# A third buffer for turned d h rows, a blockwise last store, four buffers for gate rows of s, and the gate's slope arithmetic moved to VectorE, in a gated state-space and feed-forward kernel

## The chip, the cores and the metric

The kernel runs on one core of a Trainium2 chip. The metric is the time of one execution on the device, in microseconds (us). A program on one core has no second die to compare with, so a run counts as slow only when it is over 1.5% above the fastest of its kernel. Ratios and their intervals use the other runs, the fast ones; the medians and ranges quoted beside them count every run. All profiles are of fast runs. Executions scatter: the kernel before, run 59 times beside the first experiments, had a median of 732.47 us between 726.08 and 739.44. Differences of a few us are therefore read from many rounds, never from one run.

In the lines of the profile PE is TensorE (matmuls), DVE VectorE, ACT ScalarE, POOL GpSimd and SP SyncE, which here only issues transfers; PEld is TensorE's loading of weights, and a q behind a name is that engine's queue of instructions. The span is the time from the first to the last instruction, and the granted clock is the share of TensorE's full clock that it was given.

## The reference

The program computes a gated block and all its gradients, for 2048 rows of 512 columns in bf16:

```python
def _fwd_reference(...):
    x  = A_u
    xn = _layernorm(x, axis=-1)
    s  = _A_ref(xn, A_re, A_im, B_re, B_im, C_re, C_im, log_dt, Dskip)  # long convolution + xn * Dskip
    g  = _silu(_B_ref(xn, B_w1, B_w2))     # silu(xn @ w1) @ w2, hidden width 1792
    return x + s * g

def reference(..., grad_out):
    _out, _vjp = jax.vjp(_f, A_u, A_A_re, ..., B_w1, B_w2)
    return (_out, *_vjp(grad_out))         # output and 11 gradients
```

Three pieces of the backward pass matter here. The gradient through the gate needs, for each element of the feed-forward output o, silu(o) and its slope ("gate rows"). The gradient d W1 (512 x 1792) is the product of xn with d h, the gradient of the hidden rows. It comes last, after d W2 and the gradient of the state-space part.

## The kernel before

Four parts are touched or argued about. The helper `k.st` is `nc.gpsimd.dma_start`: a store issued by GpSimd. `k.evb` casts a PSUM tile to bf16, on ScalarE in the lines shown (source line L44).

The gate rows (eight passes, two rows of tiles each). ScalarE makes silu and a tanh; GpSimd turns them into the terms of the slope; VectorE multiplies:

```python
for c in range(last):
    ...
    S = gp.tile([P, 3, 2, P], BF16, name="S", tag="S", bufs=2)
    nc.sync.dma_start(S[:]..., k.Sd[0:3, :, 256 * c:256 * c + 256]...)            # L589
    ...
    nc.scalar.activation(out=g[:], in_=src, func=ACT.Silu)                       # L593
    nc.scalar.activation(out=o, in_=src, func=ACT.Tanh, scale=0.5)               # L594
    TT(out=k.ds[:, ts, :], in0=G, in1=g[:], op=ALU.mult)                         # L595
    nc.gpsimd.tensor_scalar(out=o, in0=o, scalar1=-0.5, scalar2=0.5, ...)        # L597
    nc.gpsimd.tensor_scalar(out=g[:], in0=g[:], scalar1=1.0, scalar2=-1.0, ...)  # L598
    TT(out=o, in0=o, in1=g[:], op=ALU.mult)                                      # L599
    nc.vector.tensor_single_scalar(out=o, in_=o, scalar=1.0, op=ALU.add)         # L600
    TT(out=o, in0=o, in1=G, op=ALU.mult)                                         # L601
    ...
    TT(out=o3, in0=o3, in1=S[:], op=ALU.mult)                                    # L603
```

d W1, in seven column groups. Each needs two loads that turn (transpose) d h rows on their way from the chip's main memory, HBM. `bufs` is the number of buffers that a tile rotates through, so a load waits until the oldest one is free:

```python
for f in range(k.FT // 2):                                   # seven column groups
    dh = fw.tile([P, k.T, 2, P], BF16, name="dh_tok", tag="dh_tok", bufs=2)
    for j in range(2):
        nc.sync.dma_start_transpose(dh[:, :, j, :], k.DHd[2 * f + j])   # L949, 512 KB each
    ob = fw.tile([P, k.DK, 256], BF16, name="o10", tag="o10", bufs=2)
    for dk in range(k.DK):                                   # four blocks of 128 rows
        ps = ...
        for t in range(k.T):
            nc.tensor.matmul(out=ps[:], lhsT=k.xn[...], rhs=dh[:, t]..., ...)   # L954
        k.evb(ob[:, dk], ps[:])
        yield
    k.st(o10[:, :, 256 * f:256 * f + 256], ob[:])            # L958
```

d W2 loads h (`h_in`, L916) and turns it on TensorE (L118); its matmuls are L936. The state-space part runs beside it and loads turned rows of its own, `YT` (L725), for the matmuls L736. All these loads are issued by SyncE, one queue. The order of the end of the program is:

```python
fw = pool("fw")
dw = chained([gen_dw2(k, fw), gen_dw1(k, fw)])
paced(ssm, dw, 0.35)                                          # state-space part beside d W2
...
interleave([gen_ln_bwd(k, pool("lw", side="right")), dw], [1, 1])   # layer norm beside d W1
```

## Time and profile before

| | before |
|---|---|
| time, median of the first 3 runs (range) | 731.04 us (729.82 to 732.09) |
| span of the profiled run, mean granted TensorE clock | 728.0 us, 0.928 |
| first matmul of d W1, its length to the last matmul | 657.4 us, 62.5 us |
| from the end of the last cast to the end | 7.7 us |

The page of the profile gives busy time for each engine and then the busy share in 40 equal slices (18.2 us each) in tenths. PEclk is the granted TensorE clock in tenths of full speed:

```profile
PE 597.1 (82%) x5460; PEld 430.5 (59%) x5500; DVE 553.3 (76%) x1070; ACT 496.5 (68%) x671; POOL 107.4 (15%) x180
...
PE   0667968869999975669898999978898989988685
...
PEclk9877989989999995779899999999999999999798
```

No engine is near 100%. The last three slices, d W1, have TensorE at 6, 8 and 5 tenths and no other matmuls than these, and the sixteenth to eighteenth, the gate rows, at 5, 6 and 6. The prediction shows the lines of these two stages and of the last microseconds.

### The profile page before, as it was taken

To read this page: it belongs to the slowest core of one execution; us is meant where nothing else is said; L and a number is where in the kernel's file an instruction comes from. 1 tells how busy PE (TensorE), PEld (TensorE's weight loads), DVE (VectorE), ACT (ScalarE), POOL (GpSimd) and SP (SyncE) were. 2 spreads that over 40 slices of the span, in tenths; PEclk is the share of its full clock that TensorE was granted. 3 is DMA by queue.
4 is the path that set the end of the run, shared out by engine and by line. 5 is a ranking of instruction groups with operands and counts; after the bars stand their busy time and mean duration, and the time that the engine had idled before them with its cause. 6 is when DMAs were issued, how large, how long until landed. Compare 5 with 4: busy or idle time off the path is not lost.

```text
span 728.0 us, 13934 instructions
## 1 busy us (share of the span) xinstructions
PE 597.1 (82%) x5460; PEld 430.5 (59%) x5500; DVE 553.3 (76%) x1070; ACT 496.5 (68%) x671; POOL 107.4 (15%) x180
## 2 busy tenths in 40 slices
PE   0667968869999975669898999978898989988685
PEld 0535646555675653455575676757577767647574
DVE  6969997959978849886896999756896948369700
ACT  6767858769889866958688787646747756455221
POOL 2172200000011026600000000000002020232110
PEclk9877989989999995779899999999999999999798
DMA  9877857769769986569988975589969995379891
GB/s 291 307 171 198 248 182 207 285 146 289 299 166 285 356 267 162 186 150 261 314 208 260 240 225 193 155 221 195 236 159 246 210 259 129 110 239 209 215 216 55
DMA packets 207042, 159.26 MB, mean 219 GB/s; under 512 B 129024, under 2 KB 185344, under 8 KB 203392
## 3 DMA queue, kind: packets, MB, share of 16 engines
q1 hardware_dynamic: 193856, 135.29, 70.6%
q0 software_dynamic: 6224, 18.10, 6.9%
q10 hardware_dynamic: 6896, 4.98, 2.2%
q8 instruction: 43, 0.70, 0.4%
q14 instruction: 23, 0.19, 0.1%
HBM read 65.14 MB, written 62.26 MB: 175 GB/s over the span
## 4 chain that ended last, share of the span: by engine, by line
issue 52%; POOL 4%; DMA 3%; DVE 2%; ACT 2%; PE 1%; POOLq 0%; ACTq 0%; SPq 0%; DVEq 0%
POOL out_dram L939 1%; DMA out_dram<-gout 1%; DMA Gr<-in_grad_out_dram 1%; POOL out_dram L816 1%; DMA out_dram<-o 1%; POOL out_dram L958 1%; POOL out_dram L631 1%; DMA dB<-dA 1%; POOL out_dram L996 1%; DMA Kd<-KE 1%; ACT YD L594 1%; DVE ds L595 1%; ACT g L593 1%; DVE sp_in L332 0%; ACT dA L44 0%
## 5 line engine op out<-in xcount | busy, mean ns | idle before, releaser
L44 ACT CAST dA<-ps_s 128x1024 bf16<-128x1024 f32 x96 | 94.5, 1036 | 18.3 <-PE ps_s L298 9.8
L893 PE MATMUL ps_da<-doT,W 128*128 128x256 bf16 x448 | 61.3, 282 | 5.0 <-ACT doT L44 2.9
L310 PE MATMUL ps_i<-I,sp_in 128*128 128x256 bf16 x384 | 53.9, 287 | 13.8 <-ACT dK L44 7.0
L541 PE MATMUL ps_h<-XT,W 128*128 128x256 bf16 x448 | 63.0, 292 | 1.3 <-ACT hT L44 0.6
L44 ACT CAST o<-ps_w 128x256 bf16<-128x256 f32 (+1 forms) x42 | 18.4, 441 | 66.1 <-PE ps_w L954 38.7
L746 DVE TENSOR_TENSOR Tp<-Vb,Eb 128x1344 bf16<-128x1344 bf16 x64 | 52.1, 853 | 14.4 <-ACT Vb L44 7.6
L954 PE MATMUL ps_w<-dh_tok,xn 128*128 128x256 bf16 x448 | 52.0, 280 | 10.5 <-DMA dh_tok<-DHd 10.5
L558 PE MATMUL ps_o<-W,aT 128*128 128x512 bf16 x209 | 54.4, 393 | 4.1 <-ACT aT L549 2.9
L44 ACT CAST dB<-ps_i 128x1024 bf16<-128x1024 f32 x48 | 47.2, 1025 | 13.2 <-PE ps_i L310 10.9
L954 PEld LDWEIGHTS <-xn 128*128 128x128 bf16 x448 | 44.9, 101 | 17.7 <-issue 11.3
L310 PEld LDWEIGHTS <-sp_in 128*128 128x128 bf16 x384 | 37.4, 102 | 29.1 <-DVE sp_in L333 13.7
L893 PEld LDWEIGHTS <-W 128*128 128x128 bf16 x448 | 44.6, 101 | 15.6 <-issue 6.2
L904 PE MATMUL ps_dx<-W,dhT 128*128 128x512 bf16 x224 | 53.7, 379 | 0.0
L541 PEld LDWEIGHTS <-W 128*128 128x128 bf16 x448 | 46.0, 105 | 12.8 <-issue 2.7
L895 DVE SCALAR_TENSOR_TENSOR dhT<-dhT,ps_da 128x512 bf16<-128x512 bf16 x56 | 37.5, 683 | 16.5 <-PE ps_da L893 16.3
L936 PE MATMUL ps_w<-YD,a_tok 128*128 128x512 bf16 x211 | 49.3, 379 | 0.9 <-issue 0.3
L44 ACT CAST Vb<-ps_v 128x672 bf16<-128x672 f32 x64 | 42.3, 726 | 7.7 <-PE ps_v L736 7.7
L286 PEld LDWEIGHTS <-TF 128*128 128x128 bf16 x384 | 27.3, 104 | 24.9 <-issue 13.9
L419 ACT ACTIVATE sn<-V 128x1024 bf16<-128x1024 int32 (+3 forms) x40 | 34.8, 888 | 8.2 <-DVE V L417 8.0
L298 PE MATMUL ps_s<-dB,F 128*128 128x512 bf16 x95 | 37.9, 405 | 2.6 <-DMA dB<-dA 1.8
L297 PE MATMUL ps_s<-dB,F 128*128 128x512 bf16 x87 | 35.0, 409 | 5.4 <-DMA dB<-dA 3.5
L447 PEld LDWEIGHTS <-YD 128*128 128x128 bf16 x512 | 24.3, 101 | 24.3 <-DVE YD L434 12.7
(220 smaller groups left out, 1368.7 us busy)
## 6 DMA issues: line engine op xcount, KB each, us to landing
Yd<-YD SPq DMA_DIRECT2D x8, 1024.0 KB, 5.1
sp_in<-Ud SPq DMA_DIRECT2D x8, 1024.0 KB, 6.8
h_in<-Hd SPq DMA_DIRECT2D x14, 512.0 KB, 4.3
Ed<-E SPq DMA_DIRECT2D x8, 672.0 KB, 5.2
Eb<-Ed SPq DMA_DIRECT2D x8, 672.0 KB, 5.3
Hd<-hT POOLq DMA_DIRECT2D x8, 512.0 KB, 6.4
Ud<-dA SPq DMA_DIRECT2D x4, 1024.0 KB, 9.3
KXd<-dA SPq DMA_DIRECT2D x4, 1024.0 KB, 6.2
```

Of the source, the lines that this page charges most:

```text
L44: return self.nc.scalar.copy(out=out, in_=in_)
L297: nc.tensor.matmul(out=ps[:, 4 * u:4 * u + 4], lhsT=F2[:, m0], rhs=B[:, 0, g0:g0 + 4, :], start=True, stop=False)
L298: nc.tensor.matmul(out=ps[:, 4 * u:4 * u + 4], lhsT=F2[:, m1], rhs=B[:, 1, g0:g0 + 4, :], start=False, stop=True)
L310: nc.tensor.matmul(out=ps[:, g], lhsT=Y[:, c, g0 + g, :], rhs=k.I2[:, c].rearrange("p c m -> p (c m)"), start=(c == 0), stop=(c == 1))
L541: nc.tensor.matmul(out=ps[:, j], lhsT=k.W1[:, dk, ft * P:ft * P + P], rhs=XTv[:, :, dk, :], start=(dk == 0), stop=(dk == DK - 1))
L558: nc.tensor.matmul(out=ps[:], lhsT=aT[:, ft, t * P:t * P + P], rhs=k.W2[:, ft, :], start=(ft == 0), stop=(ft == FT - 1))
L746: k.nc.vector.tensor_tensor(out=Tp[:, c, :, r ^ c].rearrange("p e (q w) a -> p q w e a", w=2), in0=Vb[:, :, c].rearrange("p q w (e a) -> p ...
L893: nc.tensor.matmul(out=ps[:, j], lhsT=k.W2[:, ft, dk * P:dk * P + P], rhs=dTv[:, :, dk, :], start=(dk == 0), stop=(dk == DK - 1))
L895: nc.vector.scalar_tensor_tensor(out=dh[:, i0:i0 + 2, :], in0=dh[:, i0:i0 + 2, :], scalar=1.0, in1=ps[:], op0=ALU.add, op1=ALU.mult)
L904: nc.tensor.matmul(out=ps[:], lhsT=dhs[ft // 8][:, ft % 8, t * P:t * P + P], rhs=k.W1[:, :, ft * P:ft * P + P], start=(ft == 0), stop=(ft ...
L936: nc.tensor.matmul(out=ps[:], lhsT=at[:, t, :], rhs=k.do[:, t, :], start=(t == 0), stop=(t == k.T - 1))
L954: nc.tensor.matmul(out=ps[:], lhsT=k.xn[:, t, dk * P:dk * P + P], rhs=dh[:, t].rearrange("p j n -> p (j n)"), start=(t == 0), stop=(t == k ...
```

## The change

Its intent, as the diff reads, is to take away four waits. VectorE and GpSimd stop handing the slope back and forth. SyncE's queue no longer stops behind a load of S that has no buffer. TensorE no longer waits for the third group of turned d h. And the program no longer ends behind a large last store. The whole diff:

```diff
-        S = gp.tile([P, 3, 2, P], BF16, name="S", tag="S", bufs=2)
+        S = gp.tile([P, 3, 2, P], BF16, name="S", tag="S", bufs=4)
...
-        nc.gpsimd.tensor_scalar(out=o, in0=o, scalar1=-0.5, scalar2=0.5, op0=ALU.mult, op1=ALU.add)
-        nc.gpsimd.tensor_scalar(out=g[:], in0=g[:], scalar1=1.0, scalar2=-1.0, op0=ALU.mult, op1=ALU.add)
+        nc.vector.tensor_scalar(out=o, in0=o, scalar1=-0.5, scalar2=0.5, op0=ALU.mult, op1=ALU.add)
+        nc.vector.tensor_scalar(out=g[:], in0=g[:], scalar1=1.0, scalar2=-1.0, op0=ALU.mult, op1=ALU.add)
...
-        dh = fw.tile([P, k.T, 2, P], BF16, name="dh_tok", tag="dh_tok", bufs=2)
+        dh = fw.tile([P, k.T, 2, P], BF16, name="dh_tok", tag="dh_tok", bufs=3)
...
             k.evb(ob[:, dk], ps[:])
+            if f == k.FT // 2 - 1:
+                nc.sync.dma_start(o10[:, dk, 256 * f:256 * f + 256], ob[:, dk])
             yield
-        k.st(o10[:, :, 256 * f:256 * f + 256], ob[:])
+        if f < k.FT // 2 - 1:
+            k.st(o10[:, :, 256 * f:256 * f + 256], ob[:])
```

## The prediction

> **What bounds the kernel now.** I began with the page. No engine is full: TensorE is busy 82% of a 728.0 us span, VectorE 76%, ScalarE 68%, GpSimd 15%. So the kernel is a sequence of stages with different limits, and I read the three stages that the diff touches in the views of waits, of time order and of single lines. Of its 40 slices (18.2 us each) those that matter are the sixteenth to eighteenth (273 to 328 us), where the granted TensorE clock falls to 0.5 to 0.7 because TensorE starves, and the last three.
>
> First the end. This is TensorE in order of time over the last 71 us, all of it d W1 (L954):
>
> ```profile
> 657.35 14.14 PE L954 MATMUL ps_w<-dh_tok,xn 128*128 128x256 bf16 x128
> 680.18 16.61 PE L954 MATMUL ps_w<-dh_tok,xn 128*128 128x256 bf16 x128 [8.69 <-DMA dh_tok<-DHd]
> 697.87 7.15 PE L954 MATMUL ps_w<-dh_tok,xn 128*128 128x256 bf16 x64 [1.08 <-DMA dh_tok<-DHd]
> 705.76 14.13 PE L954 MATMUL ps_w<-dh_tok,xn 128*128 128x256 bf16 x128 [0.74 <-DMA dh_tok<-DHd]
> ```
>
> One of the seven column groups is 64 matmuls, 7.07 us at full clock (14.14 / 2). The brackets are idle time and its releaser: 8.69 + 1.08 + 0.74 = 10.5 us lost to turned loads. The second row takes 16.61 us where 14.14 would do: after the long wait the clock is granted at 0.50 (680.0 to 683.5) and 0.86 (683.5 to 690.0) by the view of stretches, 2.5 us more. The loads sit on SyncE's queue:
>
> ```profile
> 664.53 5.19 SPq L949 DMA_TRANSPOSE dh_tok<-DHd  x1
> 669.82 0.53 SPq L974 DMA_DIRECT2D Gt<-in_grad_out_dram  x1
> 670.44 0.38 SPq L972 DMA_DIRECT2D pd_l<-Pd  x1
> 670.87 4.74 SPq L949 DMA_TRANSPOSE dh_tok<-DHd  x1
> ```
>
> Groups 0 and 1 were loaded long before (566 to 587 us). The third group's first load is issued at 664.5, just when group 0's matmuls end (657.35 + 7.07 = 664.4): it waits for one of two buffers. The second half leaves at 670.87 and lands at 680.2, 9.3 us later.
>
> Then the last microseconds, the drains and semaphores of the program's end:
>
> ```profile
> L1175 POOLq DRAIN  x3: 40/93/6652, 720.6 to 727.7; - x3
> L1175 SPq DRAIN  x3: 7/7/7, 723.6 to 727.5; - x3
> ```
>
> The last cast ends at 720.3; GpSimd issues the last store at 720.60; it lands 2.5 us later and SyncE, which waits for it, goes on at 723.6. But GpSimd's own drain, begun behind that store, lasts 6.65 us, to 727.3, and the end barrier follows. From the last cast to the end: 7.7 us, of which about 4 are the drain alone.
>
> Last the gate rows, 262 to 317 us, as groups of instructions and as waits:
>
> ```profile
> L599 DVE TENSOR_TENSOR YD<-YD,g 128x1024 bf16<-128x1024 bf16 x8 | 8.7, 1098 | 3.3 <-POOL g L598 2.4 <-POOL YD L597 0.9
> L597 POOL TENSOR_SCALAR YD<-YD 128x1024 bf16<-128x1024 bf16 x8 | 18.5, 2315 | 22.0 <-ACT YD L594 22.0
> L598 POOL TENSOR_SCALAR g<-g 128x1024 bf16<-128x1024 bf16 x8 | 9.8, 1229 | 9.0 <-DVE ds L595 9.0
> ```
> ```profile
> ACT g L593 <- DVE YD L599: 4.3, 1, 4.3
> ```
> ```profile
> 265.28 14.58 SPq L589 DMA_DIRECT2D S<-Sd  x3
> 279.95 5.09 SPq L288 DMA_TRANSPOSE dB<-dA  x2
> ```
>
> VectorE is busy 43.9 of the 47.4 us from 268.9 to 316.3, so it is the bound there, with its waits inside. L599's shortest run is 0.68 us, its mean 1.10. The third load of S cannot issue until 279.5, when the first L603 has freed one of its two buffers, and the turned loads of dA, whose first half ScalarE finished at 276.6, stand behind it.
>
> **What the skill says.** "SBUF — State Buffer", section "SBUF: two separate sides": GpSimd and VectorE share a port pair as an exclusive lock held for the whole instruction, taken from VectorE by ops in a two-port mode or with two SBUF inputs. The trace agrees: GpSimd's L597 lasts from 1.04 up to 9.58 us and VectorE's ops have a second length, 0.7 to 0.84 us longer. "VectorE: DVE Perf Modes", "The perf-mode tier table": a bf16 scalar op in SBUF runs at four elements a cycle, tensor by tensor at two. L600 (0.41 us) against L595 (0.68) of the same size agree. "DMA: Bandwidth & Descriptors", "SWDGE vs HWDGE vs iDMA": GpSimd's transfers have their descriptors built in software on GpSimd, SyncE's in hardware. The trace shows a 0.75 us issue for the L958 store on GpSimd and 0.3 to 0.5 us for plain SyncE copies; that this is what the long drain waits for is my inference. "TensorE: Matmul & The Clock Gate", "What's actually happening": an idle TensorE falls to half clock and needs about 3.4 us of work to be warm; the 0.50 above is that.
>
> **The change part by part.**
> *Slope arithmetic.* VectorE gains 16 ops like L600: 16 x 0.41 = 6.6 us. It loses the lock contention, mean minus undisturbed time times 8: L599 3.3, L595 1.7, L603 1.7, L601 1.0, L600 0.75, together 8.4 us; and the waits for GpSimd, 2.4 + 0.9 = 3.3. So 5.1 us less for VectorE in this stage.
> *Four buffers for S.* The queue is free at 276.6 instead of 279.9, and with the earlier release of g ScalarE's 4.3 us wait shrinks by perhaps 2; the last convolution's chain starts up to 4 us earlier. This overlaps with the 5.1: VectorE's total must be done before the next stage in any case. What passes on is the smaller of the two, with some idle time where VectorE now waits for ScalarE's activations. I count 4.5 for both. It moves everything after, since the backward convolution waits for L519 (4.0 us of "PE ps_s L286 <- DVE S_b L519") and no stage after works on anything ready earlier.
> *Third buffer of turned rows.* Group 2 is loaded before 657. TensorE runs groups 0 to 2 to 678.6 without a stop, at full clock. Group 3 takes the old places of group 2 in the queue (664.5, 670.9) and lands near 680.2: 1.6 us of waiting. Group 4 (queue places at 676.8 and 681, landing 686.7) is in time for 687.3. Groups 5 and 6 wait for buffers freed at 678.6 and 687.3 and need about 6 to 8 us of issue and 6.6 of landing: some 0.5 us each. The last matmul ends at 657.35 + 7 x 7.07 + 1.6 + 1.0 = 709.5 instead of 719.9: 10.4 us.
> *Price of it.* Two more turned loads go out near 585 to 604, where SyncE's queue is nearly always issuing (3 to 5 us for each or each pair) and the transfers' share is 1.14. TensorE there is busy 90% or more and has only one wait for a load (2.6 us, h_in at 590.8). The rows of Y for the next groups have 5 to 7 us in hand. I take 2 us as lost.
> *The end in blocks.* The seventh group's four blocks of 64 KB go out on SyncE, the first three during the matmuls. After the last cast: 0.2 to start, about 2.2 to land (the 128 KB stores of Pd need 1.7 at least), 0.8 of barrier: 3.2 instead of 7.7. GpSimd's last store is then group 5's, at about 703, and its drain is over by 710. 4.5 us.
>
> Sum: 4.5 + 10.4 - 2 + 4.5 = 17.4 us, from 731.0 to 713.6.
>
> **Rivals.**
> *The turned loads themselves become the bound.* Eight of them take 33.2 us from 676.8 to 710.0 on the queue, 8.3 us a pair, against 7.07 of matmuls. For it: the rate. Against: those pairs wait for buffers; the last three pairs take 5.0 to 6.8 us. If true, the last four groups run at 8.3: 4 x 1.2 = 5 us less gain, 718 to 719.
> *VectorE takes the place of GpSimd in the gate rows*, because the 16 ops come in between its products for the convolution. For it: 43.9 of 47.4 us. Against: it loses more contention than it gains work. Then this part gives 0, 718.
> *The early load collides* with the loads of Y and h, and TensorE stops 5 us instead of 2: 717. Against: at 604 to 640 the share is 0.34 to 0.54, so there is room if the order places it there.
> *The drain is fixed* and not tied to a store just issued: then it still begins earlier, after 703, so I give this little weight. If it waits for the last cast, the end gains 1 instead of 4.5.
> *Order.* The scheduler may order other work anew; that could be some us either way.
>
> **Range and chances.** The tail's two gains (14.9) are well founded and the limit of 2% is 716.4, so one failed part leaves it near the border. Predicted 714, range 707 to 722 in 8 of 10. Faster by over 2%: 0.70; within: 0.28; slower: 0.02.
>
> **What would show it.** Waits for dh_tok of 1 to 3 us instead of 10.5, a clock of 1.0 throughout the last 70 us, last matmul 10 us nearer to the first of d W1; 3 to 4 us between last cast and end, with SyncE's store as the last to land; no GpSimd arithmetic, L599 at 0.68 us, turned loads of dA right after the casts, d W1's first matmul about 2.5 us earlier (4.5 less 2). It is wrong if a wait for dh_tok above 5 us stays, if TensorE waits longer for loads between 580 and 610, or if d W1 starts no earlier than 657.

## The result, and the profile after

The changed kernel takes 712.42 us, median of 4 runs (711.24 to 713.23), against 731.27 us for the kernel before in the same rounds. The ratio is 0.9743, with a 95% interval of 0.972 to 0.9766. Ratios here are the mean time of one kernel's fast runs over that of the other's of the same rounds, so they are not quite the ratio of the medians quoted beside them. The gain is 0.0257 x 731.27 = 18.8 us; 17.4 was predicted. The profiled run's span is 711.3 us at a mean clock of 0.947.

The same three rows of the page, now of the kernel after (slices of 17.8 us):

```profile
PE 596.8 (84%) x5500; PEld 428.8 (60%) x5500; DVE 549.4 (77%) x1086; ACT 496.5 (70%) x671; POOL 79.0 (11%) x163
...
PE   0586978879999984769669899988899998999997
...
PEclk9879998999999996779999999999989999999999
```

The three last slices are now 9, 9, 7. TensorE's total work is about unchanged (597.1 and 596.8 us busy); the gain is idle time removed. GpSimd lost 107.4 - 79.0 = 28.4 us of work, which is the two lines of slope arithmetic of before (18.5 + 9.8).

TensorE in order of time in d W1, kernel after (start, length, line, tiles, count, and in brackets the idle time before and what ended it):

```profile
657.89 28.28 PE L954 MATMUL ps_w<-dh_tok,xn 128*128 128x256 bf16 x256
686.46 7.15 PE L954 MATMUL ps_w<-dh_tok,xn 128*128 128x256 bf16 x64 [0.29 <-DMA dh_tok<-DHd]
694.09 14.13 PE L954 MATMUL ps_w<-dh_tok,xn 128*128 128x256 bf16 x128 [0.48 <-ACT o L44]
```

Four groups (256 matmuls) run without a stop, where before two did. The waits for turned loads fell from 10.5 us to 0.3, and the clock between the first and the last matmul rose from 0.92 to 1.00. The stage takes 50.3 us instead of 62.5.

SyncE's queue, kernel after (start, length of the issue, line, tiles, count):

```profile
586.04 7.18 SPq L949 DMA_TRANSPOSE dh_tok<-DHd  x2
...
665.07 4.26 SPq L949 DMA_TRANSPOSE dh_tok<-DHd  x1
...
670.49 3.89 SPq L949 DMA_TRANSPOSE dh_tok<-DHd  x1
...
675.59 20.14 SPq L949 DMA_TRANSPOSE dh_tok<-DHd  x6
703.46 5.53 SPq L958 DMA_DIRECT2D out_dram<-o  x4
```

The pair at 586 is the third group, early. The pair at 665 and 670 has the queue places of before but now belongs to the fourth group, which TensorE wants only at 657.89 + 3 x 7.07 = 679.1. The last row is the end in blocks.

The drains at the end, kernel after (engine's sequencer, count, shortest/median/longest in ns, first and last start):

```profile
L1178 POOLq DRAIN  x3: 40/93/6573, 701.9 to 711.0; - x3
L1178 SPq DRAIN  x3: 7/7/7, 710.5 to 710.8; - x3
```

GpSimd's long drain is still 6.57 us, but it begins at 701.9 behind the sixth group's store and is over at 708.5, before the last cast ends (708.6). SyncE goes on at 710.5, when its last block has landed. From the last cast to the end it is 2.7 us instead of 7.7.

The gate rows, 262 to 312 us, as groups of VectorE's instructions, kernel after (line, form, count, busy us, mean ns, idle before):

```profile
L599 DVE TENSOR_TENSOR YD<-YD,g 128x1024 bf16<-128x1024 bf16 x8 | 5.5, 685 | 0.0
...
L597 DVE TENSOR_SCALAR YD<-YD 128x1024 bf16<-128x1024 bf16 x8 | 3.4, 421 | 2.2 <-ACT YD L594 2.2
...
L598 DVE TENSOR_SCALAR g<-g 128x1024 bf16<-128x1024 bf16 x8 | 3.3, 421 | 0.0
```

L599's mean fell from 1098 to 685 ns, the undisturbed length, and its waits for GpSimd are gone. The added ops cost 3.4 + 3.3 = 6.7 us; 6.6 was predicted. Two waits of the same stretch, and SyncE's queue there:

```profile
DVE ds L595 <- DMA Gr<-in_grad_out_dram: 5.2, 1, 5.2
...
ACT g L593 <- DVE YD L599: 4.0, 1, 4.0
```

```profile
267.06 10.51 SPq L589 DMA_DIRECT2D S<-Sd  x5
277.66 4.97 SPq L288 DMA_TRANSPOSE dB<-dA  x2
```

The turned loads of dA go out 2.3 us earlier than before (279.95). VectorE still waits before its first product, 5.2 us for the gradient's rows, where it waited 6.4 before, and ScalarE's wait of 4.3 us is still 4.0.

**A first reading, which fell.** These two profiles also seemed to say something else. In the time of the span, d W1's first matmul is at 657.4 before and 657.9 after. So the gate parts appeared to bring nothing: their lead was there at 305 us, where the last convolution of the forward pass ends, and was gone when d W1 began. I formed the theory that the lead is given back between 320 and 530 us, and that the tail alone brings the gain. The rival was the prediction's own account: the gate's gain arrives in the time, and the third buffer's price hides it at this one mark. The first four experiments were made to tell these apart.

### The profile page after: what moved, and what is told of

Read it like the earlier page. It is cut to its first block, busy times and chain, and to the rows that moved or that the text cites. A ratio compares the mean times of both kernels' runs of the same rounds, so it can differ in the third digit from the quotient of the medians.

```text
span 711.3 us, 13957 instructions
## 1 busy us (share of the span) xinstructions
PE 596.8 (84%) x5500; PEld 428.8 (60%) x5500; DVE 549.4 (77%) x1086; ACT 496.5 (70%) x671; POOL 79.0 (11%) x163
## 5 line engine op out<-in xcount | busy, mean ns | idle before, releaser
L310 PE MATMUL ps_i<-I,sp_in 128*128 128x256 bf16 x384 | 51.9, 279 | 12.2 <-DVE sp_in L333 6.2
L558 PE MATMUL ps_o<-W,aT 128*128 128x512 bf16 x224 | 57.2, 394 | 2.5 <-ACT aT L549 2.0
L904 PE MATMUL ps_dx<-W,dhT 128*128 128x512 bf16 x224 | 54.4, 385 | 0.3 <-DVE dhT L895 0.3
L936 PE MATMUL ps_w<-YD,a_tok 128*128 128x512 bf16 x224 | 51.8, 379 | 0.0
L954 PE MATMUL ps_w<-dh_tok,xn 128*128 128x256 bf16 x448 | 49.6, 273 | 0.8 <-ACT o L44 0.5
L297 PE MATMUL ps_s<-dB,F 128*128 128x512 bf16 x96 | 38.6, 409 | 8.7 <-ACT dA L44 4.2
L298 PE MATMUL ps_s<-dB,F 128*128 128x512 bf16 x96 | 37.7, 399 | 1.8 <-DMA dB<-dA 1.8
```

The costliest lines, as they stand in the source:

```text
L297: nc.tensor.matmul(out=ps[:, 4 * u:4 * u + 4], lhsT=F2[:, m0], rhs=B[:, 0, g0:g0 + 4, :], start=True, stop=False)
L298: nc.tensor.matmul(out=ps[:, 4 * u:4 * u + 4], lhsT=F2[:, m1], rhs=B[:, 1, g0:g0 + 4, :], start=False, stop=True)
L310: nc.tensor.matmul(out=ps[:, g], lhsT=Y[:, c, g0 + g, :], rhs=k.I2[:, c].rearrange("p c m -> p (c m)"), start=(c == 0), stop=(c == 1))
L558: nc.tensor.matmul(out=ps[:], lhsT=aT[:, ft, t * P:t * P + P], rhs=k.W2[:, ft, :], start=(ft == 0), stop=(ft == FT - 1))
L904: nc.tensor.matmul(out=ps[:], lhsT=dhs[ft // 8][:, ft % 8, t * P:t * P + P], rhs=k.W1[:, :, ft * P:ft * P + P], start=(ft == 0), stop=(ft ...
L936: nc.tensor.matmul(out=ps[:], lhsT=at[:, t, :], rhs=k.do[:, t, :], start=(t == 0), stop=(t == k.T - 1))
```

## The experiments

Three batches, each on one chip with the kernel before in the same rounds. The medians of before were 732.47 (59 runs), 731.44 (43 runs) and 731.92 us (35 runs). Gains in us are (1 - ratio) times that median. All results were correct. Of the experiments' runs 13 were slow and are left out of the ratios: one each of the gate parts alone, the end in blocks alone and the arithmetic alone, 4 of the 20 of the third buffer alone and 6 of the 20 of the whole last store from SyncE; so were 11 of the 137 of the kernel before. On one core this rule cuts the upper end of a plain scatter, and it cuts most where one run was unusually quick. With the means of all runs instead, the third buffer alone gains 6.7 us (7.6 by the ratio) and the whole store 4.1 (5.0); the others move by 0.9 us or less.

### Undo the gate parts

```diff
 (against the kernel after)
-        S = gp.tile(..., tag="S", bufs=4)
+        S = gp.tile(..., tag="S", bufs=2)
-        nc.vector.tensor_scalar(out=o, ...)
-        nc.vector.tensor_scalar(out=g[:], ...)
+        nc.gpsimd.tensor_scalar(out=o, ...)
+        nc.gpsimd.tensor_scalar(out=g[:], ...)
```

> The changed kernel with both gate parts undone (two buffers for S, slope arithmetic on GpSimd), third buffer of turned rows and the end in blocks kept. Theory T: in the changed kernel the second L519 comes 6.5 us earlier (306.96 instead of 313.42 us) but d W1 begins at 657.89 instead of 657.35, so the gate parts' lead is given back before 520 us and is worth nothing at the end. Then this kernel takes 712 to 714 us, as the changed one does, and its d W1 begins at 657 to 659. Rival C, the prediction's: the lead of some 4.5 us carries to the end and something else of the change costs as much between 460 and 657 us. Then this kernel takes 716 to 718 us.

Measured: 719.89 us (717.91 to 726.19, 6 runs), ratio 0.9837 (0.9784 to 0.989), a gain of 11.9 us where the full change has 18.8. The interval is wide, but the time is some 7 us above the kernel after. It is above both forecasts, and near what the third buffer and the end gain alone (7.6 + 4.5 = 12.1 us, below). The theory that the gate parts bring nothing does not fit.

### The gate parts alone

```diff
 (against the kernel before)
-        S = gp.tile(..., tag="S", bufs=2)
+        S = gp.tile(..., tag="S", bufs=4)
-        nc.gpsimd.tensor_scalar(...)      # both
+        nc.vector.tensor_scalar(...)      # both
```

> The kernel before with both gate parts (four buffers for S, slope arithmetic on VectorE) and nothing else. Theory T (lead given back): second L519 near 307 us, d W1 begins at 656 to 658, time 729.5 to 731.5 us, within 0.3% of before. Rival C (lead carried): d W1 begins near 652.5, time 726 to 727 us.

Measured: 726.99 us (22 runs), ratio 0.9933 (0.9909 to 0.9957), a gain of 4.9 us. This settles it: the interval excludes no gain. Its profile has the second half of the last convolution's output (L519; count, shortest/median/longest ns, first and last start) at 305.4 us:

```profile
L519 DVE TENSOR_TENSOR S_b<-ps_i,xd x8: 1217/1225/1232, 151.7 to 305.4; 128x1024 bf16<-128x1024 f32 x8
```

In the profile of before the same instruction starts at 313.4 us, and here d W1 does begin early, at 651.4 us.

### The third buffer alone

```diff
 (against the kernel before)
-        dh = fw.tile(..., tag="dh_tok", bufs=2)
+        dh = fw.tile(..., tag="dh_tok", bufs=3)
```

> The kernel before with the third buffer of turned rows alone. All engines but SyncE keep their order of instructions, so this is the part by itself. Expected by the prediction: waits for dh_tok 1 to 3 us instead of 10.5, last matmul 10 to 12 us earlier, less 0.8 us that the two earlier loads cost at 585 to 604 us; time 719 to 721 us. Rival, the turned loads become the bound at 8.3 us a pair: 724 to 726 us.

Measured: 726.76 us (20 runs), ratio 0.9896 (0.9868 to 0.9925), a gain of 7.6 us. TensorE in d W1, third buffer alone:

```profile
663.97 21.12 PE L954 MATMUL ps_w<-dh_tok,xn 128*128 128x256 bf16 x192
685.88 7.15 PE L954 MATMUL ps_w<-dh_tok,xn 128*128 128x256 bf16 x64 [0.79 <-DMA dh_tok<-DHd]
695.31 22.79 PE L954 MATMUL ps_w<-dh_tok,xn 128*128 128x256 bf16 x192 [2.29 <-ACT pd_l L988]
```

Three groups run through, then the fourth waits 0.8 us for its load. A wait of 2.3 us for ScalarE, which was at work for the layer norm, appears in place of later waits for loads. The stage is 54.1 us.

The time missed the forecast of 719 to 721 us. The rival that would give 724 to 726 is not what happened either, since TensorE's waits for turned loads fell to 0.8 us. What the forecast left out is this wait for ScalarE and the full price of the early loads, which it put at 0.8 us (see the last section of the experiments).

### The end in blocks alone

```diff
 (against the kernel before; as in the change)
+            if f == k.FT // 2 - 1:
+                nc.sync.dma_start(o10[:, dk, 256 * f:256 * f + 256], ob[:, dk])
...
+        if f < k.FT // 2 - 1:
+            k.st(o10[:, :, 256 * f:256 * f + 256], ob[:])
```

> The kernel before with the end stored in four blocks from SyncE and nothing else. If the 6.65 us drain of GpSimd behind its last store set the end: 5 us less, 725.5 to 726.5 us, 2.5 to 3 us from the last cast to the end of the span, and the long drain over before that. Rival, the landing of the store sets the end: 1 to 1.5 us less, 729.5 to 730 us.

Measured: 726.77 us (20 runs), ratio 0.9939 (0.9913 to 0.9965), a gain of 4.5 us. From the last cast to the end: 2.7 us, as in the full change.

The three parts alone add to 4.9 + 7.6 + 4.5 = 17.0 us (16.3 with the means of all runs), and together they give 18.8, with an interval of 17.1 to 20.5. They add, as far as this can be measured.

### Within the gate: the arithmetic alone

```diff
 (against the kernel before)
-        nc.gpsimd.tensor_scalar(...)      # both; S keeps 2 buffers
+        nc.vector.tensor_scalar(...)      # both
```

> The kernel before with the slope arithmetic on VectorE alone (S keeps two buffers). The two gate parts together gave a ratio of 0.9933 (4.9 us), and their profile began d W1 6 us earlier. If the lock with GpSimd is what cost the time: 3.5 to 5 us less, ratio 0.993 to 0.995, L599 at 0.68 us. Rival, the wait of SyncE's queue for S is what cost it: 0 to 1.5 us less.

Measured: 727.23 us (22 runs), ratio 0.9929 (0.9907 to 0.995), 5.2 us: all of what the two gate parts bring together.

The trace of the kernel before shows the lock at work. Two lines of it, of GpSimd and of VectorE:

```profile
275.21 1.47 POOL L597 TENSOR_SCALAR YD<-YD 128x1024 bf16<-128x1024 bf16 x1
275.70 1.52 DVE L599 TENSOR_TENSOR YD<-YD,g 128x1024 bf16<-128x1024 bf16 x1
```

Of the 40 VectorE instructions of L595, L599, L600, L601 and L603, 11 are longer than the shortest of their line, by 0.24 to 0.85 us, and each of the 11 began while a GpSimd instruction of 1.04 to 1.47 us was under way. Of the 29 that kept their shortest length, 23 began while neither L597 nor L598 ran. The other six began inside the one L597 that lasted 9.58 us, beside a row of VectorE instructions with hardly a gap: as this reads, there it was GpSimd that was held up.

This kernel does not separate the lock from the queue by time, since the turned loads of dA went out at 275.86 us instead of 279.95 here too. But TensorE waited for these loads only 1.4 us in the kernel before, and 3.6 us in this one.

### Within the gate: the four buffers alone

```diff
 (against the kernel before)
-        S = gp.tile(..., tag="S", bufs=2)
+        S = gp.tile(..., tag="S", bufs=4)
```

> The kernel before with four buffers for S alone (arithmetic stays on GpSimd). TensorE and GpSimd keep their order. If the lock with GpSimd cost the time: 0 to 1.5 us less, with the turned loads of dA issued at 276 to 277 instead of 279.95 us but VectorE as slow as before. Rival, the queue's wait cost it: 3.5 to 5 us less.

Measured: 729.08 us (22 runs), ratio 0.9979 (0.9953 to 1.0005), 1.5 us, not clear of zero. But the queue did not become free. SyncE's queue with four buffers for S alone:

```profile
265.18 14.70 SPq L589 DMA_DIRECT2D S<-Sd  x5
279.97 4.93 SPq L288 DMA_TRANSPOSE dB<-dA  x2
```

Four loads of S go out at once, but a fifth stands before the turned loads of dA. It leaves at 279.52 us, when the first L603 ends (279.5). So these loads are as late as in the kernel before, against the forecast. In the kernels with the moved arithmetic the first L603 ends earlier (at 275.4 us in the kernel with the arithmetic alone), and that is what lets them out. This experiment therefore shows that the buffers do little. It does not test what a freer queue alone would bring.

### The third group's early loads held back

GpSimd copies two columns of the tenth h load into the third buffer before its loads may write there, so these cannot go out before that load has landed. The values copied are overwritten by the loads, so the result stays correct.

```diff
 (against the kernel after)
         nc.sync.dma_start(h[:]..., k.Hd[ft])
+        if ft == 9:
+            k.flag = fw.tile([P, 2], BF16, name="flag", tag="flag", bufs=1)
+            nc.gpsimd.tensor_copy(out=k.flag[:], in_=h[:, 0, 0:2])
...
         dh = fw.tile(..., tag="dh_tok", bufs=3)
+        if f == 2:
+            nc.gpsimd.tensor_copy(out=dh[:, 0, 0, 0:2], in_=k.flag[:])
+            nc.gpsimd.tensor_copy(out=dh[:, 0, 1, 0:2], in_=k.flag[:])
```

> The changed kernel, but the third buffer's first two turned loads are held back until the tenth load of h has landed (a two-column copy on GpSimd stands before them), so that they go out after 604 us, when the rows of Y are all loaded, instead of at 586 to 593 us. If the early loads collide with those of Y and h, as the third buffer's traces hint (d W1 begins 6 us later in three of its profiles than in two without it, and 12.2 us of gain in the last stage became 7.6 in the time): 3 to 5 us less than the changed kernel of the same rounds. Rival, those late starts are scatter of single profiles and the price is 1 us or less: within 1 us of the changed kernel. In both cases no wait for dh_tok above 1 us.

Measured: 712.16 us (6 runs), ratio 0.9728 (0.9689 to 0.9767). The loads went out at 616.8 us instead of 583 to 593, and the stretch from d W2's first matmul to d W1's fell to 102.9 us. TensorE in d W1, loads held:

```profile
655.43 21.12 PE L960 MATMUL ps_w<-dh_tok,xn 128*128 128x256 bf16 x192
679.90 29.77 PE L960 MATMUL ps_w<-dh_tok,xn 128*128 128x256 bf16 x256 [3.35 <-DMA dh_tok<-DHd]
```

Starting earlier, TensorE outruns the fourth group's loads, which still wait for the first buffer, and stands 3.35 us. Neither theory expected this wait; both had said that none would be above 1 us. The price is gone and comes back as a wait, and the time moves by no more than the intervals allow for (712.16 against 713.11 us for the kernel after on the same chip).

### The kernel after again

```diff
 (no difference from the kernel after)
```

> The changed kernel once more, on the chip of these runs, since this batch's chip may scatter more than the first. All theories: 0.972 to 0.977 of before. Its profile is a second sample of where d W1 begins: with the price of some 4 to 5 us and the gate's gain of 5 us, 656 to 660 us; the sum of the parts measured alone (4.9 gate, 7.6 third buffer, 4.5 end) is 17 us, so a ratio near 0.976.

Measured: 713.11 us (6 runs), ratio 0.975 (0.9713 to 0.9788), 18.3 us: the result repeats on another chip. TensorE's waits between 560 and 658 us (total, times, longest) in this second profile of the kernel after:

```profile
PE ps_v L736 <- DMA YT<-Yd: 2.4, 2, 1.8
PE pt_t L118 <- DMA h_in<-Hd: 1.6, 1, 1.6
```

The first of them is not in the profile before. In the first profile of the kernel after it is not there either, and the wait for h_in is 1.8 us against 2.6 before. So a single profile does not show the price of the early loads reliably. All profiles together do (see the last section of the experiments).

### The last store whole, from SyncE

```diff
 (against the kernel before)
-        k.st(o10[:, :, 256 * f:256 * f + 256], ob[:])
+        (nc.sync.dma_start if f == k.FT // 2 - 1 else k.st)(o10[:, :, 256 * f:256 * f + 256], ob[:])
```

> The kernel before with the last store of d W1 whole (256 KB), only issued by SyncE instead of GpSimd. If the long GpSimd drain behind a last GpSimd store set the end: 7.7 us from last cast to end become 3 to 4 (issue 0.4 to 0.8, landing 2.5, barrier 0.8), 4 us less in the time. Rival, cutting the store into blocks is what gave the 5.0 us: here 0 to 1 us less.

Measured: 728.23 us (20 runs), ratio 0.9932 (0.9904 to 0.996), 5.0 us, or 4.1 with the means of all runs. From the last cast to the end 3.5 us.

### The last store in blocks, from GpSimd

```diff
 (against the kernel before)
+            if f == k.FT // 2 - 1:
+                k.st(o10[:, dk, 256 * f:256 * f + 256], ob[:, dk])
...
+        if f < k.FT // 2 - 1:
+            k.st(o10[:, :, 256 * f:256 * f + 256], ob[:])
```

> The kernel before with the end in four blocks, all issued by GpSimd. If the drain sets the end, it still lasts some 6.6 us behind the last block: 7.2 to 7.7 us from last cast to end, within 0.5 us of before in the profile. Rival, the size of the last store matters: 3 to 4 us from last cast to end, 4 us less.

Measured: 732.47 us (12 runs), ratio 1.0009 (0.9979 to 1.0039): nothing. From the last cast to the end 7.7 us, as before. GpSimd's drain with blocks stored by GpSimd:

```profile
L1178 POOLq DRAIN  x3: 40/102/6681, 722.6 to 729.8; - x3
```

It begins when the last block is issued, at 722.6, and takes 6.68 us, to 729.3, though that block is a quarter of the size. So who issues the last store decides, and its size hardly does: cutting it is worth 3.5 - 2.7 = 0.8 us, taking it from GpSimd 7.7 - 3.5 = 4.2 us by the profiles.

### A fourth buffer, with the third and fourth groups' loads held

```diff
 (against the kernel with the third group's loads held)
-        dh = fw.tile(..., tag="dh_tok", bufs=3)
-        if f == 2:
+        dh = fw.tile(..., tag="dh_tok", bufs=4)
+        if f in (2, 3):
```

> The changed kernel with a fourth buffer of turned rows, the third and fourth group's loads held back until the tenth load of h has landed. With the loads out of the way, d W2's first matmul to d W1's first takes 103 us, as with two buffers, instead of 105 to 108, and the 3.4 us that the held kernel then waited for the fourth group are gone: 2.5 to 4 us less than the changed kernel, ratio to before 0.969 to 0.972. Rival, the four loads together delay those of h between 610 and 640 us: no better than the changed kernel (0.974).

Measured: 710.75 us (6 runs), ratio 0.9705 (0.9663 to 0.9746). No wait for a turned load is left in d W1. TensorE, four buffers:

```profile
651.80 21.12 PE L960 MATMUL ps_w<-dh_tok,xn 128*128 128x256 bf16 x192
673.25 3.67 PE L960 MATMUL ps_w<-dh_tok,xn 128*128 128x256 bf16 x32 [0.33 <-ACT o L44]
679.90 26.28 PE L960 MATMUL ps_w<-dh_tok,xn 128*128 128x256 bf16 x224 [2.98 <-ACT o L44]
```

A wait of 3.0 us for a cast by ScalarE takes its place, and the stretch from d W2's first matmul to d W1's is 104.5 us where 103 was expected. This is the lowest median of all kernels run, 0.4 to 0.5% below the kernel after by the ratios, but the intervals overlap: it is probably better, not shown to be.

### More buffers for the output rows

In the kernel after, ScalarE waits 9.8 us and VectorE 5.0 us between 330 and 385 us for rows of the output stage, waits that were smaller before (0.6 and 2.5). If they cost the part of the gate's lead that is lost after 305 us, more buffers should bring it back.

```diff
 (against the kernel after)
-        S = pool.tile(..., tag="go_s", bufs=2)      # go_g likewise
+        S = pool.tile(..., tag="go_s", bufs=3)
-    q = [load(0), load(1)]
+    q = [load(c) for c in range(3)]
-        x = pool.tile(..., tag="go_x", bufs=1)
+        x = pool.tile(..., tag="go_x", bufs=2)
-    out = gen_out(k, da)
+    out = gen_out(k, pool("go", side="right", es=es_x))
     paced(bwd, woven([ffb, out], [2, 1]), BR)
+    run(out)
     es_x.close()
...
-    run(out)                  # later; and load(c + 2) becomes load(c + 3)
```

> The changed kernel with a third buffer and earlier loads for the rows of the output's last step (gate row, S, x), whose loads ScalarE and VectorE wait for in order between 335 and 400 us (9.8 and 5.0 us at 336 to 380 in the changed kernel, 0.6 and 2.5 in the kernel before). Over the profiles the gate's lead is 7.7 us at the second L519 and 5.0 at the first matmul on turned rows of Y. If those waits give back the 2.7 us: 2 to 3 us less than the changed kernel (0.970 to 0.972). Rival, TensorE and VectorE are simply full in that stage: within 1 us of it, 0.973 to 0.976.

Measured: 715.99 us (6 runs), ratio 0.9785 (0.9745 to 0.9825): not faster than the kernel after. The waits of this kernel, 330 to 385 us:

```profile
ACT go_g L627 <- DMA go_g<-Od: 7.5, 2, 3.9
...
DVE go_x L630 <- DMA go_x<-in_A_u_dram: 3.9, 2, 2.4
```

They shrank by 2.3 and 1.1 us without a gain. The edit also reordered TensorE's instructions, so it does not settle whether these waits matter. Nor is the loss of time against the kernel after made here: d W1 begins at 657.1 us, as there (657.9 and 657.4), but then TensorE waits 2.7 us for the fourth group's turned load, where the kernel after waited 0.3 and 0.5. The experiment gives no support to the theory and does not refute it.

### What the marks of all profiles say together

| kernel | first d W1 matmul | d W2's first to d W1's first | d W1's length | last cast to end |
|---|---|---|---|---|
| before | 657.4 | 104.1 | 62.5 | 7.7 |
| gate parts alone | 651.4 | 103.2 | 63.7 | 7.7 |
| third buffer alone | 664.0 | 104.3 | 54.1 | 7.7 |
| gate parts undone | 663.9 | 107.1 | 50.5 | 2.7 |
| after | 657.9 | 105.5 | 50.3 | 2.7 |
| after, again | 657.4 | 107.6 | 50.2 | 2.7 |
| third held | 655.4 | 102.9 | 54.2 | 2.7 |
| four held | 651.8 | 104.5 | 54.4 | 2.7 |

The averages below use the profiles of the other experiments too. d W1's first matmul, averaged over profiles: 659.0 us with neither the moved arithmetic nor the early third group (5 profiles, 656.4 to 662.2), 651.9 with the arithmetic alone (2), 663.9 with the early third group and no moved arithmetic (2), 657.6 with both (2). The two parts pull this mark in opposite directions and nearly cancel in the kernel after. That is what the first reading took for a gain given back. The sizes of these shifts are rough: the two profiled runs with the arithmetic alone were 2.1 and 4.8 us quicker than the medians of their kernels.

The price of the early loads has a part that no wait shows. The stretch from d W2's first matmul to d W1's, first in the kernel before, then in the kernel after (the stretch, its length, busy us of PE, PEld, DVE, ACT and POOL, then the granted clock, the transfers' share and GB/s):

```profile
553.20:657.40 104.20, 97.20 (x1007) 67.91 (x1018) 66.64 (x178) 62.26 (x89) 21.87 (x41) 1.00 0.81 193
552.40:657.90 105.50, 99.82 (x1020) 69.44 (x1017) 67.39 (x180) 62.36 (x89) 21.96 (x41) 0.98 0.85 201
```

The granted clock of this stretch is 0.98 in four of the five profiles with an early third group (all but the third buffer alone), and 1.00 in all nine without one. In the kernel after it is 0.50 from 592 to 594 us, just after a wait of 1.8 us for h. The kernel before waited 2.6 us at that place and kept 1.00, so the wait by itself does not explain it; what lowers the clock stays open. Waits for `YT`, 1.0 to 2.4 us in all, appear in four of these five profiles too (all but the first of the kernel after), and in none of the nine.

## Why the prediction was right

The time was 712.4 us where 714 was predicted, within the range. The kernel is faster by over 2%. Step by step:

**Slope arithmetic and buffers for S (4.5 us predicted).** Right in size: 4.9 us alone, with an interval of 3.2 to 6.7. The mechanism is the first half of the step: the lock contention and the hand-over to GpSimd go, as L599's 685 ns show. How much of the gain is due to each was not separated. This agrees with the Trainium skill's "SBUF — State Buffer", "SBUF: two separate sides", on the shared port, and with "VectorE: DVE Perf Modes", "The perf-mode tier table": the added scalar ops took 421 ns and the products of the same size 685. The rival that VectorE takes GpSimd's place and the part gives 0 fell with the 4.9 us. The second half failed, in size and in mechanism. The four buffers alone bring 1.5 us with an interval that reaches past zero, and they do not free the queue: the turned loads of dA left at 279.97 us, not 276.6, because a fifth load of S still stood before them. The moved arithmetic let them out instead (275.86 us without the buffers). So 4.5 for both is right partly by luck: it was taken as the smaller of two gains of which one is not there. The step also expected ScalarE's wait of 4.3 us to shrink by 2; it stayed at 4.0. The gain at the end of the stage is larger than predicted: the last L519 comes at 305.8 us on average over six profiles with the moved arithmetic and at 313.7 over seven without, 7.9 us. At the first matmul on YT it is 5.0 us (483.4 against 488.4). So 3 us are lost in between, against the step's claim that the lead moves everything after. The prediction had allowed for loss by idle time, but in the gate stage itself. Where they go is open: the kernel with more buffers for output rows was made to show it and did not.

**Third buffer (10.4 us predicted, less 2).** Right. d W1's length is 61.7 us on average over the seven profiles with two buffers, and 51.3 over four with the early third group: 10.4 us (the kernel with more buffers for output rows, whose order is another, is left out of these averages). That the tenths agree is luck: the four lie between 50.2 and 54.1 us, and the step's own sum gives 709.5 - 657.35 = 52.1. In its terms it was less exact. The step put 1.6 us of waiting at the fourth group and 0.5 at the last two each. The kernel after waited 0.3 us, at the fifth, and in its second profile 0.5 us, at the fourth. The third buffer alone waited 0.8 us at the fourth and then 2.3 for ScalarE. The price, 2 us, measured 2.7: the stretch from d W2's first matmul to d W1's is 103.4 us on average with two buffers (seven profiles, 102.4 to 104.1) and 106.1 with the early third group (four, 104.3 to 107.6). Both marks lie in one profile, so shifts from earlier stages do not enter. Holding the third group's loads brought it down to 102.9. The step was wrong about where the price lies. It looked for waits alone, and took TensorE as busy 90% or more, where its own view has 16.93 of the 20 us from 580 to 600. A good part is the lower clock: of the profiles with the same number of matmul records there (1015), the five without early loads have TensorE busy for 98.3 us, the kernel after for 100.0. The net of the two marks, 10.4 - 2.7 = 7.7, agrees with the 7.6 us of the third buffer alone, or 6.7 with the means of all runs.

**The rival of a load rate of 8.3 us a pair** fell. The last three pairs were issued in 20.14 us, 6.7 a pair with their waits for buffers inside, and TensorE did not wait for the last two.

**The end in blocks (4.5 us predicted).** Right in size, 4.5 us alone and 7.7 - 2.7 = 5.0 by the profiles, and right in its reason: GpSimd's drain follows its last store. The landing after the last cast was put at 2.4 us and took 1.9 (708.6 to 710.5). The rival of a fixed drain fell: it starts with GpSimd's last store, at 701.9 us in the kernel after, and not with the last cast. The description "in blocks" is the smaller half, as the two kernels that separate the queue from the cut show. The inference that the long drain waits for descriptors built in software remains one: the runs show that it is tied to GpSimd's last store and nearly independent of its size, not what it does.

**The tests that failed were the prediction's own.** It said that it would be wrong if d W1 started no earlier than 657 us, and 2.5 us earlier was expected. The two profiles after have 657.9 and 657.4, and still the time came out as forecast. Profiles of four kernels that do the same up to that point (before and the three that change only the end) differ by 3.8 us there (656.4 to 660.2), so a shift of 2.5 us cannot be read from one profile of each. The averages have 659.0 - 657.6 = 1.4 us. It would also be wrong if TensorE waited longer for loads between 580 and 610 us: it waited 2.6 us before, 1.8 in the first profile after and 4.0 in the second, so this test gives two answers. What told the truth were timed runs of the parts and intervals inside one stage.

## What to carry to other kernels

In this program a last store issued by GpSimd cost 4 to 5 us over one issued by SyncE: check the drains after the last useful instruction, and try another queue. A further buffer for a load at the start of a stage is worth the wait that it removes less what the earlier load costs where it now goes out, and both can be measured between two marks of one profile, the clock included. A further buffer frees a queue only if it covers every load that stands before the one you want: look at the queue in the profile of that part alone. When parts of a change pull the same mark in opposite directions, the mark stays still: time each part alone before calling one of them useless.

## What the Trainium skill lacked or had wrong

- "VectorE: DVE Perf Modes", "The DRAIN you can't avoid", knows two kinds of drain: the flush after each VectorE instruction, and the runtime's boilerplate before and after a program, about 12 ns and constant on all five engines. What it lacks is a drain like GpSimd's long one here, the first of three at the line that ends the program (L1175 before, L1178 after): 6.57 us in the kernel after, 6.65 in the one before and 6.68 with small blocks, always behind its last store. SyncE's three at that line are 7 ns each. When GpSimd's store is the last, its drain sets the end: moving the store to SyncE took 4.2 us off the end in the profiles and 5.0 us (4.1 with the means of all runs) off the time.
- "DMA: Bandwidth & Descriptors", "Latency and other measured facts", gives turned transfers a bandwidth of 261 GB/s where the middle dimension is not contiguous, 2.0 us for 512 KB (an estimate from that figure), and more where it is. It has nothing on how long one load of this size from HBM holds the issuing queue. Here a single 512 KB turned load held SyncE's queue 3.9 to 4.3 us (the two at 665 and 670 us in the kernel after).
- I found no page that says how far the marks of two profiles of one kernel lie apart. Here it was 3.4 us at the first matmul on YT between two profiles of the kernel after (485.0 and 481.6 us), with spans of 711.3 and 710.7.
